# First chunk of an attention + expert-MLP kernel: second products in float32r from the fifth hidden tile, other places for two tiles' split weights, one subtraction moved to GpSimd

## The chip, the cores and the metric

One core of a Trainium2 chip runs the kernel. The metric is the device time in microseconds (us), median over runs of one build; an execution also has a profile, whose span (first to last recorded instruction) is a little shorter than its time.

## The reference

```python
scores = q @ k.T / sqrt(64)                      # 8 batches x 8 heads, 576 positions, head_dim 64
# heads 0-3: rel = pos_q - pos_k in [0, 32);  heads 4-7: rel in [0, 128) and rel % 4 == 0; else -1e9
attn = exp(scores - max) / (sum + 1e-9)
x = (attn @ v)  ->  (4608 tokens, 512)
h = x @ w_in                                     # 512 -> 2048
g = where(h > 0, h, exp(min(h, 0)) - 1)
out = g @ w_out                                  # 2048 -> 512
```

All inputs are float32 or wider; the MLP's weights come to the chip as 64-bit words.

## The kernel before

**Order of the work.** The attention of batch 0 is done first. Then the MLP goes through the tokens in chunks of 512 (chunks 0, 1 and 2), and what is left in larger pieces with combined weights. This case is about **chunk 0**, some 40 to 130 us into the span. It has 16 hidden tiles f = 0..15 of 128 features. For each f TensorE makes `product1(0, f)`, h = x times w_in of tile f, into one of two PSUM banks (`h0`, `h1`, in turn); ScalarE (ACT) and VectorE (DVE) make the ELU of it: ACT Exp (L627), ACT Relu (L629), DVE (L632 or L634). Two tiles later (`LAG` = 2) `second_product(0, f)` multiplies it with w_out of tile f and adds into four PSUM banks `o_ps0..3`. Attention of batch 1 (`second_attention`) runs between the tiles: scores into PSUM (`a_ps`), masks added by DVE (L397), maximum (L410, L413), Exp on ACT (L389), sums and reciprocal on DVE (L326, L327), the multiplication by them on GpSimd (POOL, L328), transposes on DVE (L432), copies into `pt` by ACT and POOL (L435), then products with v into `a_ps`.

**Weights.** A raw pair of weight tiles (w_in of one tile, w_out of another) is loaded into `r0`..`r3` and made float32 in `a0`..`a7`: ACT L136 (`magnitude`), then DVE L144, L152, L154 (`convert`, `upper_and_lower`).

**Two forms of a product.** In plain float32 one product is one matmul that TensorE runs in several passes. In float32r (F32R) each operand is split into a high part and a rest, and three matmuls (high·high, high·rest, rest·high) do the work. The split of a weight is `split_steps`: ACT casts (L191), a vector engine subtracts (L193). The split of an activation is `parts` in `elu`: ACT casts `gh` (L642), DVE subtracts `gl` (L643). First products of chunk 0 are float32r from f = `F1` = 3, second products from f = `F2` = 6. `split_w(k, t0, t1)` splits tile t0..t1 of pair k; called after tile f with k = f + 1 and t0 = 0 it splits w_in of tile f + 2, with t0 = 1 it splits w_out of tile f.

**Where the split weights go.** `places_of(k)` gives the two places: for k < 6 two buffers of a small pool (`brief`, of names `gl` or `h`), for 6 ≤ k < 8 a buffer `a-1`, later ones `r0` to `r2`. w_out of tiles below 11 goes to `brief("e")` or `brief("h")`.

**Order on the engines.** Matmuls keep the order of the program; on the other engines a scheduler fixes the order of the instructions when the kernel is built, from its own estimate of when each is ready (`schedule_with_timeline_sim=True`). On the chip each engine then runs its list strictly in order, and an instruction that waits holds all behind it. `tc.issue_after` adds a wanted order for single pieces.

Of the kernel before, what the change touches and what calls it, by code (L numbers as in the profile page):

```python
# [36 lines left out]
NE = 2  # L37
LAG = 2
F1 = 3
F2 = 6  # L40
NEG = -1.0e9
HT = DM // 2
TH = 384
# [31 lines left out]
def body(ctx: ExitStack, tc: tile.TileContext, q, k, v, masks, w_in, w_out, out):  # L75
    nc = tc.nc
# [82 lines left out]
    def room_of(name):  # L159

        if name not in taken:
            taken[name] = wst.tile([P, 4 if name[0] == "a" else 8, DM], F32 if name in PLAIN else F32R, name=name[:3].rstrip("'"))
        return taken[name]

    def slots(name, *at):

        step = at[1] - at[0] if len(at) > 1 else 1
        return room_of(name)[:, at[0]:at[-1] + 1:step, :]

    def brief(name):  # L170

        return [fp.tile([P, TC], F32R, name=name, bufs=4 if name == "e" else 2).unsqueeze(1) for _ in range(2)]

    def places_of(k, t0, t1):

        if k < 6:
            return brief("gl" if k % 2 else "h")
        if k < 8:
            o = (k - 6) * 2
            return slots("a-1", o), slots("a-1", o + 1)  # L180
        if k < 12:
            o = (k - 8) * 2
            return slots("r0", o), slots("r0", o + 1)
        o = k % 2 * 2
        return slots(f"r{1 + (k - 12) // 2}", o, o + 4), slots(f"r{1 + (k - 12) // 2}", o + 1, o + 5)

    def split_steps(k, t0, t1, places=None, v=nc.vector, a=nc.scalar):

        h, l = places or places_of(k, t0, t1)
        w = full2[k][:, t0:t1, :]  # L190
        a.copy(out=h, in_=w)  # L191
        yield
        v.tensor_tensor(out=l, in0=w, in1=h.bitcast(F32), op=ALU.subtract)  # L193
        for t in range(t0, t1):
            wh[need[2 * k + t]], wl[need[2 * k + t]] = h[:, t - t0, :], l[:, t - t0, :]

    def split_w(*args):

        for _ in split_steps(*args):
            pass  # L200
# [108 lines left out]
    def copies(b, hp, places, keep=lambda ins: ins):  # L309

        for a_ps, n0, n1 in places:
            flat, q0, q1 = a_ps[:, :(n1 - n0) * QB], n0 * QB, n1 * QB
            if hp >= NPAIR // 2:
                last = keep(nc.scalar.copy(out=x32[b][:, hp, q0:q1], in_=flat))
            else:
                dst = x32[b][:, hp, :].rearrange("p (c u) -> p c u", c=DIL)[:, :, q0 // DIL:q1 // DIL]
                last = keep(nc.scalar.copy(out=dst.rearrange("p c (s i) -> p s c i", i=G // DIL),
                                           in_=flat.rearrange("p (s c i) -> p s c i", c=DIL, i=G // DIL)))
        return last
# [258 lines left out]
    def split_x(c, v=nc.vector, a=nc.scalar, between=None):  # L578
        for hp in range(NC):
            if between is not None and hp == NC - 2:  # L580
                between()
            xh[hp], xl[hp] = xall[:, 2 * hp, :], xall[:, 2 * hp + 1, :]
            t0 = c * TC
            while t0 < (c + 1) * TC:
                b, o = divmod(t0, S)
                n = min(S - o, (c + 1) * TC - t0)
                u = slice(t0 - c * TC, t0 - c * TC + n)
                src = x32[b][:, hp, o:o + n]
                last_cast = a.copy(out=xh[hp][:, u], in_=src)
                last = v.tensor_tensor(out=xl[hp][:, u], in0=src, in1=xh[hp][:, u].bitcast(F32), op=ALU.subtract)  # L590
                t0 += n
        return last.ins, last_cast.ins
# [27 lines left out]
    def elu(h_ps, c, f, v=nc.vector, a=nc.scalar):  # L620
# [7 lines left out]
        if c == 0:  # L628
            below.append(nc.scalar.activation(out=e, in_=e, func=AF.Relu, scale=-1.0, bias=1.0).ins)  # L629
            if f < F2:  # L630
                g = fp.tile([P, TC], F32, name="gh", bufs=3)
# [353 lines left out]
    for c in range(CS):  # L985
        if c == 1:
            last_x = split_x(c, vec, act, lambda: copies(*last_outputs, inorder))
            pend.append((0, NF - 2, next(ends[0])))
            split_w(NF - 1, 0, 2, None, vec, act)
            next(ends[1])  # L990
            next(ends[1])
            pend.append((0, NF - 1, next(ends[1])))
            split = 1
        elif c > 1:
            split_x(c)
        if c == 1:
            for j in (14, 15, 12, 13, *range(12)):
                keep_whole(j)
        when = WHEN.get(c, ())
        for f in range(NF):  # L1000
            while c == 0 and ready < min(NF, f + AHEAD):
                for j in (ready, ready + 1):
                    with tc.issue_after(below[-1] if below else last_copy.ins):
                        magnitude(j)
                if f > 0:
                    with tc.issue_after(last_conversion.ins):
                        last_conversion = convert(ready // 2, behind=maxima[-1] if maxima else None)
                for j in (ready, ready + 1):
                    if j + 2 * NR < NF:
                        load_w(j + 2 * NR)  # L1010
                ready += 2
            if c == 0 and f == F1 - 2:
                with tc.issue_after(masked[-1] if masked else last_step[NPAIR - 1]), tc.issue_after(below[-1]):
                    split_x(0)
            while c == 1 and split < min(12, f + 2):
                with tc.issue_after(last_transpose[1] if split < 2 else last_x[0]), tc.issue_after(low[NF - 3 - F2] if split < 2 else last_x[1]):
                    with tc.issue_after(low[-1]), tc.issue_after(high[-1]):
                        split_late(split)
                split += 1
            strict = (vec, act) if c == CS - 1 and f >= LAST else ()  # L1020
            if c == 0 and f >= NF - 2:
                ends.append(elu_steps(gemm1(c, f)))
                if f == NF - 2:
                    next(ends[0])
                    first_late = split_steps(0, 0, 2, [slots(*a) for a in LATE[0]], vec, act)
                else:
                    for _ in first_late:
                        pass
                    next(ends[0])
            else:  # L1030
                parts = elu(gemm1(c, f), c, f, *strict)
                if parts is not None:
                    pend.append((c, f, parts))
            if c == 1:
                keep_plain(f)
            if (c, f) == (0, 0):

                for part in slice(0, 2 * DM), slice(2 * DM, 4 * DM):
                    with tc.issue_after(last_conversion.ins), tc.issue_after(hidden[-1]):
                        last_conversion = convert(1, part=part)  # L1040
            if c == 0 and F1 <= f + 2 < NF:

                with tc.issue_after(hidden[-2]):
                    split_w(f + 1, 0, 2 if f >= 11 else 1)
                    if F2 <= f < 11:
                        split_w(f + 1, 1, 2, brief("e" if f % 2 else "h"))
            if c == 0:
                with tc.issue_after(hidden[-1] if f > 1 else last_step[NPAIR - 1]):
                    last_outputs = next(att)
                if f == NF - 2:  # L1050
                    next(first_late)
            if (c, f) == (CS - 1, EARLY):
                made[0] = scores_piece(CS + 1, (0, 1), lambda: flush(LAG))
                credit[0] -= 6.0
            flush((LAG - 1 - (f == NF - 1) if c == 0 and f >= NF - 2 else LAG if c < CS - 1 or f < NF - 1 else LAG + 1) - len(waiting))
            if (c, f) in COMBINE:
                with tc.issue_after(low[-1]), tc.issue_after(high[-1]):
                    combine(COMBINE[c, f])
            if f in when:
                i = when.index(f)  # L1060
                if i % 2 == 0:
                    made[i] = scores_piece(c + 1, (i, i + 1))
                else:
                    outputs_piece(made.pop(i - 1))
            if (c, f) == (CS - 1, OPER):
                take_places()
                for what in SOON:
                    moving_operand(0, what, vec, act)
            if (c, f) == (CS - 1, OPER + 1):
                for what in THEN:  # L1070
                    moving_operand(0, what, vec, act)
# [67 lines left out]
```

## Time and profile before

| what | value |
|---|---|
| median of 3 runs | 872.69 us (871.42 to 872.86) |
| profiled execution | 872.5 us, span 870.7 us (1.8 us around it), mean granted clock 0.996 |
| TensorE (PE) busy | 853.7 us, 98% of the span |
| DVE, ACT, POOL busy | 555.7 (64%), 526.9 (61%), 75.0 us (9%) |

The profile has one row for each engine's instructions. In a timeline row the columns are the start in us from the span's start, the length of the group in us, the engine, the source line, the operation, what is written from what, the tile size, and the number of instructions in it. A square bracket at the end is the idle time of that engine ahead of the row, and what ended it. PE is TensorE's matmul stream.

### The profile page before, as it was taken

The numbers are of one execution on the slowest core, as the hardware profiler recorded it, in microseconds if no ns is written. First come the engines' busy times: TensorE is split into PE (matmuls) and PEld (weight loads), VectorE is DVE, ScalarE is ACT, GpSimd is POOL, SyncE is SP. The second block draws the span as 40 slices with busy tenths as digits, with TensorE's granted clock in tenths as the row PEclk, the third lists the DMA queues.
The fourth block names the chain that finished last, engine by engine and source line by source line (L and its number), as shares of the span: only waits on it lengthen the run. The fifth ranks groups of instructions, "written<-read, shape, count | busy, mean of one in ns | idle before, by whom it ended". The sixth has DMA issues, their size and how long they took to land.

```text
span 870.7 us, 17559 instructions
## 1 busy us (share of the span) xinstructions
PE 853.7 (98%) x6788; PEld 722.5 (83%) x6788; DVE 555.7 (64%) x902; ACT 526.9 (61%) x1031; POOL 75.0 (9%) x112
## 2 busy tenths in 40 slices
PE   6999999999999999999999999999999999999998
PEld 4556878888878889888878898988899988999986
DVE  6899987766685857787765577545476635344431
ACT  3767987756585756667654575654566654555541
POOL 2013311000020200111010020100011100000000
PEclk8999999999999999999999999999999999999999
DMA  9997335134546346867753867662875652776441
GB/s 343 378 381 264 132 123 188 34 132 133 176 160 200 102 151 215 262 221 239 231 173 100 279 200 242 212 184 83 265 226 175 206 164 80 241 209 191 143 153 56
DMA packets 93459, 166.48 MB, mean 191 GB/s; under 512 B 9696, under 2 KB 40768, under 8 KB 93376
## 3 DMA queue, kind: packets, MB, share of 16 engines
q1 hardware_dynamic: 89200, 158.01, 57.0%
q10 hardware_dynamic: 4176, 7.34, 2.3%
q8 instruction: 54, 0.88, 0.4%
q14 instruction: 29, 0.24, 0.1%
HBM read 124.42 MB, written 40.89 MB: 190 GB/s over the span
## 4 chain that ended last, share of the span: by engine, by line
PE 84%; DVE 7%; ACT 4%; DMA 2%; issue 2%; POOL 1%; SPq 0%; ACTq 0%; DVEq 0%; POOLq 0%
PE o_ps L111 41%; PE h L111 34%; PE a_ps L111 8%; DVE a L152 1%; DMA out<-e 1%; POOL pt L435 1%; DVE a L154 1%; DMA r<-combined 1%; DVE nmx L410 1%; ACT sm L389 0%; ACT pt L383 0%; DVE sm L397 0%; PE a L111 0%; DMA kt<-k 0%; DVE a L144 0%
## 5 line engine op out<-in xcount | busy, mean ns | idle before, releaser
L111 PE MATMUL h<-xall,r 128*128 128x384 f32 (+1 forms) x708 | 156.9, 363 | 0.4 <-DVE e L634 0.2
L111 PEld LDWEIGHTS h<-xall,r 128*128 128x128 f32 x708 | 127.7, 188 | 17.2 <-issue 0.8
L111 PE MATMUL o_ps<-a,gh 128*128 128x512 f32 x394 | 129.0, 416 | 0.0
L448 DVE SCALAR_TENSOR_TENSOR a-1_3369<-a-1_3369,a 128x768 f32<-128x768 f32 x64 | 61.0, 953 | 87.9 <-ACT a L448 87.9
L111 PE MATMUL h<-r,r 128*128 128x384 f32 x476 | 108.3, 337 | 0.4 <-DMA r<-combined 0.4
L448 ACT COPY e<-h 128x384 f32<-128x384 f32 x96 | 46.0, 479 | 98.5 <-PE h L111 96.6
L111 PEld LDWEIGHTS o_ps<-a,gh 128*128 128x128 f32 x394 | 73.4, 188 | 21.8 <-issue 9.1
L448 ACT ACTIVATE a<-a-1_3369 128x384 f32<-128x384 f32 (+1 forms) x96 | 60.8, 634 | 50.0 <-DVE a-1_3369 L448 44.0
L111 PEld LDWEIGHTS h<-r,r 128*128 128x128 f32 x476 | 84.4, 188 | 4.0 <-ACT e L448 0.7
L111 PE MATMUL o_ps<-r,gh 128*128 128x512 f32 x242 | 75.4, 393 | 0.0
L111 PE MATMUL o_ps<-a,r 128*128 128x512 f32 x288 | 72.3, 392 | 0.0
L111 PE MATMUL o_ps<-a,gl 128*128 128x512 f32 x173 | 67.7, 391 | 0.0
L448 ACT ACTIVATE a<-a 128x768 f32<-128x768 f32 (+1 forms) x72 | 60.8, 845 | 1.9
L111 PEld LDWEIGHTS o_ps<-a,r 128*128 128x128 f32 x288 | 53.7, 188 | 9.9
L111 PE MATMUL h<-a,r 128*128 128x384 f32 x256 | 60.1, 336 | 0.0
L448 DVE TENSOR_TENSOR a-1_3369<-h,e 128x384 f32<-128x384 f32 x64 | 35.2, 550 | 34.8 <-PE h L111 34.7
L111 PEld LDWEIGHTS o_ps<-r,gh 128*128 128x128 f32 x242 | 44.9, 188 | 8.6
L111 PEld LDWEIGHTS h<-a,r 128*128 128x128 f32 x256 | 46.4, 188 | 4.2
L111 PE MATMUL o_ps<-r,gl 128*128 128x512 f32 x117 | 46.0, 393 | 0.2 <-DVE gl L448 0.2
L435 POOL COPY pt<-sm 32x384 f32<-32x384 f32 x36 | 32.9, 913 | 103.1 <-DVE sm L432 102.1
L111 PE MATMUL o_ps<-a,xall 128*128 128x512 f32 x153 | 39.5, 393 | 0.0
L637 DVE SCALAR_TENSOR_TENSOR e<-h,e 128x512 f32<-128x512 f32 x30 | 20.9, 696 | 27.1 <-ACT e L636 27.1
(219 smaller groups left out, 1553.6 us busy)
## 6 DMA issues: line engine op xcount, KB each, us to landing
r<-combined SPq DMA_DIRECT2D x224, 256.0 KB, 3.6
aside<-a-1_3369 SPq DMA_DIRECT2D x64, 192.0 KB, 3.4
vt<-v SPq DMA_DIRECT2D x30, 384.0 KB, 4.4
kt<-k SPq DMA_DIRECT2D x30, 304.0 KB, 4.9
qt<-q SPq DMA_DIRECT2D x30, 288.0 KB, 4.2
r<-w_in SPq DMA_DIRECT2D x16, 512.0 KB, 7.9
r<-w_out SPq DMA_DIRECT2D x16, 512.0 KB, 8.3
combined<-a SPq DMA_DIRECT2D x20, 256.0 KB, 3.2
```

Source lines behind the costliest of these rows:

```text
L111: return inorder(nc.tensor.matmul(*args, **kw))
L152: keep(nc.vector.scalar_tensor_tensor(out=au, in0=hi, scalar=0x80000000, in1=au, op0=ALU.bitwise_and, op1=ALU.bitwise_or))
L154: return keep(nc.vector.scalar_tensor_tensor(out=au, in0=lo, scalar=29, in1=au, op0=ALU.logical_shift_right, op1=ALU.bitwise_or))
L410: nc.vector.tensor_reduce(out=nmx, in_=sm, op=ALU.max, axis=mybir.AxisListType.X)
L435: last_transpose[b] = (nc.gpsimd.tensor_copy if r else nc.scalar.copy)(out=tr[ks, :, cs], in_=sm[cs, :, rs]).ins
L448: return lambda *args, **kw: inorder(getattr(self.eng, name)(*args, **kw))
L637: v.scalar_tensor_tensor(out=e, in0=h_ps, scalar=0.0, in1=e, op0=ALU.max, op1=ALU.subtract)
```

## The change

`F2` goes from 6 to 4, so second products of tiles 4 and 5 are float32r too; their w_out is split into a buffer that later holds `a6` (`slots("a6''", ...)`). The splits of w_in of pairs k < 6 go into a buffer that later holds `a7` (`slots("a7''", ...)`) and no longer into the pool's. The subtraction for w_in of the fourth tile (f = 3, called after tile 1 = `F1` - 2) is issued to GpSimd and no longer to DVE.

```diff
-F2 = 6
+F2 = 4
...
         if k < 6:
-            return brief("gl" if k % 2 else "h")
+            o = k % 2 * 2
+            return slots("a7''", o), slots("a7''", o + 1)
...
                 with tc.issue_after(hidden[-2]):
-                    split_w(f + 1, 0, 2 if f >= 11 else 1)
+                    split_w(f + 1, 0, 2 if f >= 11 else 1, None, nc.gpsimd if f == F1 - 2 else nc.vector)
                     if F2 <= f < 11:
-                        split_w(f + 1, 1, 2, brief("e" if f % 2 else "h"))
+                        o = f % 2 * 2
+                        split_w(f + 1, 1, 2, (slots("a6''", o), slots("a6''", o + 1)) if f < 6 else brief("e" if f % 2 else "h"))
```

In the built program line numbers grow by 1 below L176 (by 2 in the last lines). Three places show how the order on the engines moves. Numbers behind names tell buffers apart.

**DVE, tiles 3 to 5**, from the ELU of tile 3 to that of tile 5 (`gh`, `e` by L632/L633, L634/L635: the ELU; `a2`, `a3`: weights being converted; L193/L194: rests of weights; `sm`, `a_ps`: attention). Before:

```order
L632 SCALAR_TENSOR_TENSOR gh_704<-h1_688,e_701 128x512
L144 TENSOR_SCALAR a3_769<-a3_769 128x2048
L193 TENSOR_TENSOR h_707<-a2_638,h_706 128x512
L193 TENSOR_TENSOR gl_799<-a2_638,gl_798 128x512
L432 STREAM_TRANSPOSE sm_619<-sm_619 96x12x32 x2
L632 SCALAR_TENSOR_TENSOR gh_796<-h0_780,e_793 128x512
L397 TENSOR_TENSOR sm_748<-a_ps0_710,masks_sb_76 96x384
L397 TENSOR_TENSOR sm_748<-a_ps1_711,masks_sb_76 96x384
L632 SCALAR_TENSOR_TENSOR gh_839<-h1_823,e_836 128x512
```

With the change:

```order
L633 SCALAR_TENSOR_TENSOR gh_701<-h1_685,e_698 128x512
L144 TENSOR_SCALAR a3_764<-a3_764 128x2048
L194 TENSOR_TENSOR a7_577<-a2_637,a7_577 128x512
L194 TENSOR_TENSOR a6_798<-a2_637,a6_798 128x512
L433 STREAM_TRANSPOSE sm_618<-sm_618 96x12x32 x2
L194 TENSOR_TENSOR a7_577<-a2_637,a7_577 128x512
L635 SCALAR_TENSOR_TENSOR e_788<-h0_775,e_788 128x512
L644 TENSOR_TENSOR gl_793<-e_788,gh_792 128x512
L398 TENSOR_TENSOR sm_743<-a_ps0_705,masks_sb_76 96x384
L398 TENSOR_TENSOR sm_743<-a_ps1_706,masks_sb_76 96x384
```

Between the ELU of tile 4 and the mask additions now stands `gl` of tile 4 (and ACT's cast for it), and one more rest lies ahead.

**DVE, tiles 10 and 11**, where `gl_1133` (before) and `gl_1153` (with the change) belong to tile 10, `gl_1172` and `gl_1192` to tile 11. Before:

```order
L634 SCALAR_TENSOR_TENSOR e_1128<-h0_1115,e_1128 128x512
L193 TENSOR_TENSOR h_1139<-a5_990,h_1138 128x512
L154 SCALAR_TENSOR_TENSOR a6_1109<-r2_644,a6_1109 128x2048
L643 TENSOR_TENSOR gl_1133<-e_1128,gh_1132 128x512
L634 SCALAR_TENSOR_TENSOR e_1167<-h1_1154,e_1167 128x512
L397 TENSOR_TENSOR sm_1216<-a_ps0_1178,masks_sb_76 96x384
L397 TENSOR_TENSOR sm_1216<-a_ps1_1179,masks_sb_76 96x384
L144 TENSOR_SCALAR a7_1249<-a7_1249 128x2048
L193 TENSOR_TENSOR r1_1175<-a6_1109,r1_1175 128x2x512
L410 TENSOR_REDUCE nmx_1219<-sm_1216 96x12
L193 TENSOR_TENSOR r1_1175<-a6_1109,r1_1175 128x2x512
L643 TENSOR_TENSOR gl_1172<-e_1167,gh_1171 128x512
```

With the change:

```order
L194 TENSOR_TENSOR h_1159<-a5_1010,h_1158 128x512
L154 SCALAR_TENSOR_TENSOR a6_1129<-r2_643,a6_1129 128x2048
L635 SCALAR_TENSOR_TENSOR e_1148<-h0_1135,e_1148 128x512
L635 SCALAR_TENSOR_TENSOR e_1187<-h1_1174,e_1187 128x512
L398 TENSOR_TENSOR sm_1236<-a_ps0_1198,masks_sb_76 96x384
L398 TENSOR_TENSOR sm_1236<-a_ps1_1199,masks_sb_76 96x384
L144 TENSOR_SCALAR a7_1269<-a7_1269 128x2048
L194 TENSOR_TENSOR r1_1195<-a6_1129,r1_1195 128x2x512
L411 TENSOR_REDUCE nmx_1239<-sm_1236 96x12
L194 TENSOR_TENSOR r1_1195<-a6_1129,r1_1195 128x2x512
L644 TENSOR_TENSOR gl_1153<-e_1148,gh_1152 128x512
L644 TENSOR_TENSOR gl_1192<-e_1187,gh_1191 128x512
```

`gl` of tile 10 moves from ahead of the mask additions to behind both wide rests, directly ahead of `gl` of tile 11.

**ACT, start of chunk 1** (`L624 COPY h<-h0` takes h of a tile out of the one PSUM bank that chunk 1 uses for it; L418 is the Exp of an attention; L678 copies results out). Before:

```order
L642 CAST gh_1662<-e_1497 128x512
L191 CAST a6_1695<-a1_538 128x1024
L624 COPY h_1660<-h0_1646 128x512
L627 ACTIVATE e_1659<-h_1660 128x512
L678 COPY e_1674<-o_ps0_680 128x512
L418 ACTIVATE sm_1593<-sm_1593 96x768
L678 COPY e_1680<-o_ps1_682 128x512
```

With the change:

```order
L643 CAST gh_1682<-e_1517 128x512
L192 CAST a6_1715<-a1_538 128x1024
L419 ACTIVATE sm_1613<-sm_1613 96x768
L625 COPY h_1680<-h0_1666 128x512
L628 ACTIVATE e_1679<-h_1680 128x512
L679 COPY e_1694<-o_ps0_677 128x512
L679 COPY e_1700<-o_ps1_679 128x512
```

The attention's Exp now stands ahead of the copy of h of tile 1 of chunk 1; before it stood three instructions behind it.

## Rows read from the trace of the kernel before

**Rows 1.** The page: busy time by engine, and the busy tenths of PE and DVE in 40 equal slices of the span (21.8 us each).

```profile
PE 853.7 (98%) x6788; PEld 722.5 (83%) x6788; DVE 555.7 (64%) x902; ACT 526.9 (61%) x1031; POOL 75.0 (9%) x112
...
PE   6999999999999999999999999999999999999998
...
DVE  6899987766685857787765577545476635344431
```

**Rows 2.** Busy time by stretch of chunk 0. Columns: stretch, length, busy us (and instructions) of PE, PEld, DVE, ACT, POOL, then granted clock, DMA share, GB/s.

```profile
44.00:62.00 18.00, 16.96 (x126) 10.38 (x124) 16.77 (x21) 11.91 (x37) 2.97 (x4) 1.00 1.01 378
62.00:84.00 22.00, 21.71 (x161) 13.69 (x160) 21.25 (x24) 18.31 (x48) 5.80 (x3) 1.00 0.79 281
84.00:113.00 29.00, 29.00 (x214) 23.57 (x213) 27.29 (x34) 22.29 (x54) 9.55 (x6) 1.00 0.44 147
113.00:135.00 22.00, 21.77 (x132) 17.24 (x131) 17.94 (x28) 18.85 (x54) 3.52 (x4) 1.00 0.34 109
```

**Rows 3.** Timeline of PE, tiles 3 to 7: the first product of tile 3 (in two rows, the wait between them), the attention's product with v, then first product of tile 6, second of tile 4, first of tile 7, second of tile 5.

```profile
44.48 2.11 PE L111 MATMUL h<-xall,h 128*128 128x512 f32 x8
47.63 1.19 PE L111 MATMUL h<-xall,h 128*128 128x512 f32 x4 [1.03 <-DVE h L193]
...
62.56 1.23 PE L111 MATMUL a_ps<-pt,vt 128*64 128x96 f32 x24 [0.29 <-PE h L111]
...
66.85 3.31 PE L111 MATMUL h<-xall,gl 128*128 128x512 f32 x12
70.00 3.59 PE L111 MATMUL o_ps<-a,gh 128*128 128x512 f32 x8
73.03 3.30 PE L111 MATMUL h<-xall,a-1_841 128*128 128x512 f32 x12
...
77.16 3.70 PE L111 MATMUL o_ps<-a,gh 128*128 128x512 f32 x8
```

**Rows 4.** Timeline of PE, second products of tiles 10 (from 107.80) and 11 (from 113.24), with the first use of `gl` in each, and first products of tiles 13 and 14.

```profile
107.80 0.61 PE L111 MATMUL o_ps<-h,gh 128*128 128x512 f32 x2
108.25 0.39 PE L111 MATMUL o_ps<-h,gl 128*128 128x512 f32 x1
...
110.52 2.88 PE L111 MATMUL h<-xall,r 128*128 128x512 f32 x12
113.24 0.62 PE L111 MATMUL o_ps<-r,gh 128*128 128x512 f32 x2
113.70 0.39 PE L111 MATMUL o_ps<-r,gl 128*128 128x512 f32 x1
...
116.38 3.01 PE L111 MATMUL h<-xall,r 128*128 128x512 f32 x12 [0.23 <-DVE e L634]
```

**Rows 5.** Timeline of DVE: the maximum and the rest around 45 us, ELU of tile 4, mask additions, `gl` of tile 10, the ELU of tile 11 directly behind it, and `gl` of tile 11; the brackets are all waits of DVE over 0.2 us from 44.30 to 112.78.

```profile
44.30 0.94 DVE L410 TENSOR_REDUCE nmx<-sm 96x12 f32<-96x768 f32 x1
...
46.89 0.68 DVE L193 TENSOR_TENSOR h<-a,h 128x512 fp32r<-128x512 f32 x1
...
60.06 0.65 DVE L632 SCALAR_TENSOR_TENSOR gh<-h,e 128x512 f32<-128x512 f32 x1
61.91 1.02 DVE L397 TENSOR_TENSOR sm<-a_ps,masks_sb 96x384 f32<-96x384 f32 x2 [1.20 <-POOL pt L435]
63.60 0.69 DVE L632 SCALAR_TENSOR_TENSOR gh<-h,e 128x512 f32<-128x512 f32 x1 [0.67 <-ACT e L629]
...
85.66 1.02 DVE L397 TENSOR_TENSOR sm<-a_ps,masks_sb 96x384 f32<-96x384 f32 x2 [0.95 <-POOL pt L435]
...
95.75 0.69 DVE L634 SCALAR_TENSOR_TENSOR e<-h,e 128x512 f32<-128x512 f32 x1 [0.65 <-ACT e L629]
...
106.38 0.68 DVE L643 TENSOR_TENSOR gl<-e,gh 128x512 fp32r<-128x512 f32 x1
106.98 0.68 DVE L634 SCALAR_TENSOR_TENSOR e<-h,e 128x512 f32<-128x512 f32 x1
...
112.78 0.67 DVE L643 TENSOR_TENSOR gl<-e,gh 128x512 fp32r<-128x512 f32 x1
```

**Rows 6.** Timeline of POOL in chunk 0: two multiplications of the attention, tensor operations with two inputs.

```profile
55.43 1.47 POOL L328 TENSOR_TENSOR sm<-sm,sums 96x768 f32<-96x768 f32 x1 [35.05 <-DVE sums L327]
...
94.55 1.89 POOL L328 TENSOR_TENSOR sm<-sm,sums 96x768 f32<-96x768 f32 x1 [8.92 <-DVE sums L327]
```

**Rows 7.** Timeline of DVE: an instruction that lies beside the first of these, and one of the same kind that has none of POOL's multiplications beside it.

```profile
55.72 2.26 DVE L144 TENSOR_SCALAR a<-a 128x2048 uint32<-128x2048 uint32 x1
...
80.80 1.20 DVE L144 TENSOR_SCALAR a<-a 128x2048 uint32<-128x2048 uint32 x1
```

**Rows 8.** Timeline of ACT: the cast of w_in of tile 3, the first conversion for `a6`, and three rows of the start of chunk 1.

```profile
43.81 0.62 ACT L191 CAST h<-a 128x512 fp32r<-128x512 f32 x1 [1.15 <-DVE a L154]
...
95.62 2.16 ACT L136 ACTIVATE a<-r 128x1024 f32<-128x1024 f32 x2
...
140.51 0.59 ACT L624 COPY h<-h 128x512 f32<-128x512 f32 x1 [0.69 <-PE h L111]
...
143.13 0.85 ACT L418 ACTIVATE sm<-sm 96x768 f32<-96x768 f32 x1 [0.89 <-DVE sm L417]
143.88 0.56 ACT L678 COPY e<-o_ps 128x512 f32<-128x512 f32 x1
```

**Rows 9.** Timeline of PE: first product of tile 2 of chunk 1.

```profile
143.03 2.88 PE L111 MATMUL h<-xall,r 128*128 128x512 f32 x12
```

## The prediction

> **What bounds the kernel now.** Read first the busy shares [rows 1]: PE is busy 98% of the span, so the program as a whole is bound by TensorE, and a saving of matmul time counts unless something else is late. The slices in tenths in the same group speak against reading the change off that average: DVE stands at 9, 9, 8, 7, 7, 7 and 6 in the slices from the third on, which is chunk 0, and at 3 to 5 at the end. The table by stretch shows it closer [rows 2]: DVE is busy 16.77 of 18.00 us, 21.25 of 22.00 and 27.29 of 29.00, that is 93 to 97% up to 113 us; PE in the same stretches loses 1.04, 0.29 and 0 us. Two engines are full there, and PE is the one that sets the pace only by a little. How little is seen by following DVE to where PE uses its results: PE uses `gl` of tile 11 at 113.70, and DVE had it ready at 112.78 + 0.67 = 113.45, 0.25 us earlier; `gl` of tile 10 was ready at 107.06 and used at 108.25, 1.19 us earlier [rows 4, 5]. So the question is less what PE is spared than what DVE gets to do between 44 and 113 us, and in which order.
>
> The predicted sum is made against the profiled execution, 872.5 us, 0.2 us below the median of the three runs (872.69). About 0.2%, 1.74 us, is what a measurement of this kernel can tell from no change.
>
> **The change, part by part.**
>
> *A. Second products of tiles 4 and 5 in float32r: PE −1.5 us.* A first product and the float32 second product after it take 73.03 − 66.85 = 6.18 us [rows 3]; a second product in float32r and the first product after it 113.24 − 107.80 = 5.44 us [rows 4]. That spares 0.74 us a tile, 1.48 us for two.
>
> *B. The fourth tile's rest on GpSimd: the wait of 1.03 us goes, and comes back 15 us later: 0.* PE waits 1.03 us at 46.6 for DVE's rest of w_in of tile 3, which DVE only makes at 46.89 [rows 3, 5]. GpSimd is idle there and can start when ACT's cast ends, 43.81 + 0.62 = 44.43 [rows 8]. No subtraction of this size by GpSimd is in the trace; its multiplications of 96x768 took 1.47 to 1.89 us [rows 6], so for 512 elements per partition in place of 768 I estimate 0.98 to 1.26 us, and take 0.98; as bounds stand 0.6 (DVE's own pace) and the whole 1.89. Even at 1.89 the rest is there at 46.3, before PE needs it at 44.48 + 2.11 = 46.59. So the wait goes. But at 62.56 the attention's product with v had already to wait 0.29 us, and it writes the banks that DVE's mask additions read until half of 1.02 us behind 61.91, i.e. 62.42 [rows 3, 5]. PE can come there a microsecond earlier; it only gains if the mask additions do too. In the new order DVE's transposes end one subtraction (0.60 us, the step from 106.38 to 106.98) earlier, but then come one more rest, the ELU of tile 4 (done at about 60.7, as now at 60.06 + 0.65), then `gl` of tile 4, which has to wait for ACT's cast of 0.62 us: 60.7 + 0.1 + 0.62 = 61.4, plus 0.67 for itself, gives 62.05 as the start of the mask additions in place of 61.91. Nothing is gained there: B is 0 for the span.
>
> *The places: 0.* The buffer of `a6` is wanted by ACT's conversion only at 95.62 [rows 8], that of `a7` later; the last readers of the new places are the first product at 66.85 and the second product at 77.16 [rows 3], which end some 15 us and more before. Were that cover gone, the conversion of 2.16 us, and ACT's casts behind it, would wait for them. No DMA is added or removed. ACT's four more casts of 0.62 us (`gh` of tiles 4 and 5, w_out of 4 and 5), 2.5 us, are hidden in the 6.1 us it idles from 44 to 62 and the 3.7 us from 62 to 84 [rows 2], but for the one cast above.
>
> *C. DVE has more to do, and `gl` of tile 10 is put last: +5.8 us.* DVE gets four subtractions (rests of w_out 4 and 5, `gl` of 4 and 5) and loses one (w_in of tile 3). I count by the lists of instructions. From the maximum at 44.30 on, what stands ahead of `gl` of tile 10 in the new list is what stood ahead of `gl` of tile 11 in the old one, plus one rest and one `gl` of 128x512 (the other two of the four take the place of the w_in rest that went and of `gl` of tile 10 itself). So `gl` of tile 10 starts where tile 11's did, 112.78, plus 2 × 0.60 = 1.20, plus the change in DVE's waits. Those were 1.20 + 0.67 + 0.95 + 0.65 = 3.47 us [rows 5]. In the new order I expect 0.75 (`gl` of tile 4 behind its cast, above; the first two waits go, since the work now lies in them), 0.95 (as before), and 1.3 at the transposes near 96, which wait for GpSimd's multiplication of 1.89 us [rows 6] with only one ELU of 0.6 between: together about 3.05, 0.4 less. `gl` of tile 10 then starts at 112.78 + 1.20 − 0.4 = 113.6 and is ready at 114.25; PE can use it at 114.3. Before it used it at 108.25. PE therefore is 6.06 us late at that place, whatever it gained ahead of it (A and B only make the wait there longer). Of this 0.23 us comes back, since before's wait of 0.23 at 116.38 [rows 4] is covered then. Net +5.8 us. Bounds: if all of DVE's waits vanished, `gl` would start at 112.78 + 1.20 − 3.47 = 110.5 and be used at 111.2, +2.9 and net +2.7; if all stayed as before and DVE lost 0.6 more beside GpSimd, 114.6 as a start, 115.3 as use, +7.1 and net +6.8. I take 5.8, nearer the upper end, because the rows with the waits are ones that the new order keeps or replaces by like ones.
>
> *D. Start of chunk 1: ACT's Exp ahead of a copy: +1.5 us.* Chunk 1 has one PSUM bank for h, so the first product of tile 2 waits for ACT's copy of tile 1's h. Before, that copy ran at 140.51 to 141.10, and the product at 143.03 didn't wait [rows 8, 9]. Now the Exp of an attention, which waited for DVE and ran at 143.13 to 143.98, stands ahead of it. The copy would take the slot behind it, 143.88 to 144.47, and the product start at 144.5 in place of 143.03. Bounds: 0 (the Exp ready earlier relative to PE, as PE comes late into this chunk by C) and 143.88 − 140.51 = 3.4 (the copy late by that, nothing hidden). I take 1.5.
>
> Sum: 872.5 + 5.8 + 1.5 = **879.8 us**; the ends of C and D give 875.2 (with 2.7 and 0) to 882.7 (with 6.8 and 3.4). Late next behind C is tile 11: its `gl` comes directly behind, so it costs nothing more.
>
> *A rule weighed.* By the rows, DVE does wait beside GpSimd: L144 took 2.26 us at 55.72, while GpSimd multiplied from 55.43 to 56.90, and 1.20 us at 80.80 with no multiplication beside it [rows 6, 7]. The Trainium skill, page "SBUF — State Buffer", section "Who interferes with whom", says that a DVE instruction with two SBUF inputs contends with a GpSimd instruction that reads SBUF, and that whoever is first holds the shared ports for the whole instruction while the other is blocked; the rows agree. By that rule the moved subtraction, if it lasts to 45.5, blocks nothing, and if to 46.3, it holds DVE's conversion at 45.76 for 0.5 us: the sum would be 879.8 or 880.3.
>
> **Rivals.**
>
> *Faster: PE sets the pace all the way (870.0 us).* If DVE keeps up, A and B are kept: 872.5 − 1.48 − 1.03 = 870.0. It is one mechanism, DVE's lead over PE at tile 10: it decides by whether `gl` of tile 10 is ready when PE, 2.5 us earlier, wants it, 108.25 − 2.5 = 105.75. For it: PE's saving is sure, and DVE loses a rest early. Against: DVE's slack at tile 11 was 0.25 us, three subtractions net come on top, and the order puts `gl` of tile 10 behind 5.8 us of work that was behind it before (106.98 to 112.78). Chance 0.11.
>
> *Level: only the added work counts, not the order (872.9 us).* If the waits give DVE room, so that it is at `gl` of tile 10 in time, and only tile 11 is late: ready at 112.78 + 1.20 − 0.4 + 0.67 = 114.25 with 114.31 as first use against 113.70: +0.6, less the 0.23: 872.9. For it: this is where the backlog alone would hit. Against: each engine runs its list in order, so the place of `gl` of tile 10 counts. Chance 0.09.
>
> *Heavier (883 to 886 us).* GpSimd and DVE hold each other up as in [rows 7] (0.5 to 1), D goes to its 3.4, and what ACT does for chunk 1 is late once more (1 to 3). 872.5 + 6.8 + 3.4 = 882.7 and above. Chance 0.10.
>
> *The change does nothing*, because float32r in tiles 4 and 5 is hidden anyway, is in the level case.
>
> **How the numbers follow.** Forecast 0.70 (879.8; its own range 875.2 to 882.7), faster 0.11, level 0.09, heavier 0.10. The range leaves out the faster case, half of the level one and the upper part of the heavier one, some 2 in 10: 873.0 to 883.5. Faster by over 0.2%: 0.11; within it: 0.09; slower: 0.80.
>
> **What would show it.** In the changed profile: no wait of PE at 46.6, and a GpSimd subtraction of 128x512 of about 1 us from 44.5 on (B); PE waiting 0.3 to 1.5 us ahead of the product with v near 62.6, for DVE (B is 0); second products of tiles 4 and 5 in rows of two and one float32r matmuls in place of one row of x8 (A); DVE at 95% or more between 44 and 113; the largest wait of PE in chunk 0, some 3 us, at the first use of `gl` of tile 10 near 113 to 114 (C); a wait of PE of 1 to 2 us for ACT's copy in chunk 1, near 150 (D). C is wrong if that wait isn't there, or if tile 10's second product has begun its third matmul before 111; D is wrong if no wait for L625 is over 0.5 us beyond before's.

## The result, and the profile after

| | median | runs | ratio to before (95% interval) |
|---|---|---|---|
| before | 872.74 us | 871.42 to 872.86 | |
| with the change | 883.34 us | 882.9 to 884.47 | 1.0122 (1.0106 to 1.0138) |

The change makes the kernel 10.6 us slower; 879.8 was predicted, with a range of 873.0 to 883.5. The measured time lies 0.16 us below the upper end of that range. The profiled execution took 882.9 us, its span is 881.1 us, 10.4 more than before.

The page of the changed kernel, busy time by engine and the busy tenths of PE and DVE, answers to [rows 1]:

```profile
PE 856.4 (97%) x6796; PEld 725.6 (82%) x6796; DVE 558.9 (63%) x905; ACT 530.1 (60%) x1035; POOL 72.3 (8%) x113
...
PE   6989989999999999999999999999999999999998
...
DVE  6899977757585866787765476645466646344331
```

In chunk 0, PE has two slices of 8 now where it had 9. The table by stretch answers to [rows 2]:

```profile
44.00:62.00 18.00, 17.60 (x126) 10.37 (x124) 17.95 (x21) 12.64 (x38) 4.66 (x4) 1.00 1.01 382
62.00:84.00 22.00, 19.81 (x159) 14.26 (x160) 21.06 (x25) 17.41 (x47) 5.46 (x6) 0.92 0.77 261
84.00:113.00 29.00, 26.79 (x201) 20.78 (x199) 27.69 (x34) 24.90 (x59) 4.80 (x5) 1.00 0.47 162
113.00:135.00 22.00, 19.68 (x108) 15.73 (x110) 14.82 (x20) 13.03 (x42) 3.27 (x4) 0.92 0.29 96
```

DVE is busy 17.95 of 18.00 us and 21.06 of 22.00, PE stands still for 2.2 to 2.3 us in each of the three later stretches, and the granted clock, 1.00 throughout before, is 0.92 on the mean in two of them. The timeline of PE shows where (all its waits of over 0.2 us in chunk 0, with the rows behind two of them, and the two at the start of chunk 1), to be read against [rows 3, 4, 9]:

```profile
47.19 1.21 PE L111 MATMUL h<-xall,a 128*128 128x512 f32 x4 [0.22 <-POOL a L194]
...
64.19 1.26 PE L111 MATMUL a_ps<-pt,vt 128*64 128x96 f32 x24 [2.36 <-DVE sm L398]
65.37 5.30 PE L111 MATMUL o_ps<-a,gh 128*128 128x512 f32 x8
70.11 3.32 PE L111 MATMUL h<-xall,a 128*128 128x512 f32 x12
...
105.52 0.50 PE L111 MATMUL o_ps<-e,gl 128*128 128x512 f32 x1 [0.78 <-DVE gl L644]
...
108.93 3.06 PE L111 MATMUL h<-xall,r 128*128 128x512 f32 x12 [0.86 <-DVE e L635]
111.82 0.61 PE L111 MATMUL o_ps<-h,gh 128*128 128x512 f32 x2
115.32 0.50 PE L111 MATMUL o_ps<-h,gl 128*128 128x512 f32 x1 [2.88 <-DVE gl L644]
...
118.84 3.36 PE L111 MATMUL h<-xall,r 128*128 128x512 f32 x12
122.04 0.61 PE L111 MATMUL o_ps<-r,gh 128*128 128x512 f32 x2
...
152.50 3.06 PE L111 MATMUL h<-xall,r 128*128 128x512 f32 x12 [1.08 <-ACT h L625]
...
159.36 3.01 PE L111 MATMUL h<-xall,a 128*128 128x512 f32 x12 [1.07 <-ACT h L625]
```

The second product at 65.37 takes 4.74 us up to the next row, where the same one took 66.85 − 63.72 = 3.13 in the kernel before:

```profile
63.72 3.70 PE L111 MATMUL o_ps<-a,gh 128*128 128x512 f32 x8
```

Busy time hides this: PE counts as busy for the whole of the 4.74 us. The table in stretches of 1 and 2 us behind the two long waits shows the clock (third number from the end):

```profile
65.00:66.00 1.00, 1.00 (x11) 0.71 (x8) 0.96 (x2) 1.00 (x2) 0.00 (x0) 0.61 0.65 232
66.00:67.00 1.00, 1.00 (x2) 0.34 (x1) 0.99 (x2) 1.00 (x4) 0.00 (x0) 0.50 0.50 98
67.00:68.00 1.00, 1.00 (x2) 0.34 (x1) 1.00 (x1) 1.00 (x8) 0.00 (x0) 0.50 0.75 272
...
116.00:118.00 2.00, 2.00 (x8) 1.53 (x7) 2.00 (x3) 1.50 (x7) 0.00 (x0) 0.60 0.18 60
118.00:120.00 2.00, 2.00 (x7) 1.57 (x6) 1.59 (x3) 2.00 (x14) 0.00 (x0) 0.54 0.03 8
120.00:122.00 2.00, 2.00 (x10) 1.68 (x9) 2.00 (x2) 1.11 (x8) 0.00 (x0) 1.00 0.00 0
```

About a microsecond after each of the two waits the clock goes from 2.4 to 1.2 GHz (0.50), for some 3.5 us. What the other engines did there: GpSimd's subtraction, DVE's conversion beside it, `gl` of tile 4, the mask additions, `gl` of tiles 10 and 11; and ACT at the start of chunk 1 (answering to [rows 5, 8]):

```profile
44.85 2.28 POOL L194 TENSOR_TENSOR a<-a,a 128x512 fp32r<-128x512 f32 x1 [24.13 <-ACT a L192]
```

```profile
46.10 2.11 DVE L152 SCALAR_TENSOR_TENSOR a<-r,a 128x1024 uint32<-128x1024 uint32 x1
...
62.75 0.71 DVE L644 TENSOR_TENSOR gl<-e,gh 128x512 fp32r<-128x512 f32 x1 [0.68 <-ACT gh L643]
63.39 1.01 DVE L398 TENSOR_TENSOR sm<-a_ps,masks_sb 96x384 f32<-96x384 f32 x2
...
114.58 1.28 DVE L644 TENSOR_TENSOR gl<-e,gh 128x512 fp32r<-128x512 f32 x2
```

```profile
151.13 0.84 ACT L419 ACTIVATE sm<-sm 96x768 f32<-96x768 f32 x1 [3.79 <-DVE sm L418]
151.89 0.56 ACT L625 COPY h<-h 128x512 f32<-128x512 f32 x1
```

`gl` of tiles 10 and 11 run back to back from 114.58, with no idle time of DVE ahead of them. ACT stands 3.79 us behind DVE, and the copy that PE needs stands behind that Exp.

**How late PE is, mark by mark.** TensorE's products come in the same order in all kernels here (f adds twelve matmuls to one of them), so a product's start can be set against its start in the trace of before. The table gives the difference in us, less the difference at 44.48 (which lies ahead of the change and is −0.1 to 1.0).

| start in before, and what starts | change | a | b | c | e | f | g | h | j | k |
|---|---|---|---|---|---|---|---|---|---|---|
| 62.56 product with v | 1.28 | 0.86 | 0.41 | 0.42 | 1.28 | 1.29 | 0.70 | 0.30 | 0.00 | 0.00 |
| 66.85 first product 6 | 2.91 | 0.84 | 0.41 | 0.42 | 2.96 | 2.92 | 0.70 | 0.30 | 0.00 | −0.01 |
| 107.80 second product 10 | 3.67 | 2.31 | 0.41 | 0.46 | 3.68 | 3.62 | 0.29 | −0.01 | 1.01 | 1.04 |
| 113.24 second product 11 | 8.45 | 7.48 | 0.41 | 2.17 | 3.68 | 6.84 | 4.25 | −0.01 | 2.67 | 1.04 |
| 140.31 chunk 1, behind first product 1 | 7.88 | 6.93 | −0.14 | 1.61 | 4.79 | 6.27 | 3.67 | 1.13 | 2.12 | 2.43 |
| 154.39 chunk 1, first product 4 | 10.18 | 7.12 | −0.34 | 1.14 | 7.71 | 8.57 | 3.95 | 0.65 | 1.64 | 2.62 |

In the column of the change, 4.8 us come from second product 10 to second product 11 (the wait and the half clock behind it), and 2.3 at the start of chunk 1. Behind 154.39 it stays as it is.

### The profile page after: what moved, and what is told of

It reads as the page before. It is cut to its first block, busy times and chain, and to the rows that moved or that the text cites. A ratio compares the mean times of both kernels' runs of the same rounds, so it can differ in the third digit from the quotient of the medians.

```text
span 881.1 us, 17581 instructions
## 1 busy us (share of the span) xinstructions
PE 856.4 (97%) x6796; PEld 725.6 (82%) x6796; DVE 558.9 (63%) x905; ACT 530.1 (60%) x1035; POOL 72.3 (8%) x113
## 4 chain that ended last, share of the span: by engine, by line
PE 85%; DVE 6%; ACT 5%; issue 2%; DMA 1%; SPq 0%; POOL 0%; ACTq 0%; DVEq 0%
PE o_ps L111 41%; PE h L111 35%; PE a_ps L111 8%; DVE a L152 1%; DMA kt<-k 1%; DVE a L144 1%; ACT pt L384 0%; DVE sm L398 0%; ACT sm L390 0%; DVE a L194 0%; DVE nmx L411 0%; ACT a L136 0%; ACT pt L436 0%; ACT gh L643 0%; ACT a L192 0%
## 5 line engine op out<-in xcount | busy, mean ns | idle before, releaser
L111 PE MATMUL o_ps<-a,gl 128*128 128x512 f32 x181 | 70.8, 391 | 0.0
L111 PEld LDWEIGHTS o_ps<-a,gl 128*128 128x128 f32 x181 | 34.0, 188 | 7.1
```

The source lines that it names most:

```text
L111: return inorder(nc.tensor.matmul(*args, **kw))
```

## The experiments

The theory (L): PE is set by when DVE reaches `gl` of tile 10 in its list; then come the half clock behind long waits and ACT's list at the start of chunk 1. Its rivals put the loss on GpSimd (G), on the amount of DVE's work alone (W), on PE's lost time adding up from the front (P), or on the places.

**a: the rest of tile 4 on DVE again.**

```diff
-                    split_w(f + 1, 0, 2 if f >= 11 else 1, None, nc.gpsimd if f == F1 - 2 else nc.vector)
+                    split_w(f + 1, 0, 2 if f >= 11 else 1)
```

> The change with the subtraction of the fourth tile's rest back on DVE. Theory L (the list of DVE): the time is set by where DVE's list puts the gl of tile 10, and by what PE's long waits cost behind it; GpSimd's part is small. DVE gets 0.60 us back to do and loses the 0.90 us that its conversion was held at 46.1. PE's largest wait of chunk 0, near 112 to 115, stays over 2 us. 881 to 885 us. Rival G (GpSimd): the subtraction on GpSimd, 2.28 us where 0.98 was estimated, and the hold of DVE beside it make most of the loss; without it 873 to 877 us.

Measured: 879.4 us, ratio 1.0073 (1.0055 to 1.0092). Both numbers missed. The rows of PE, of DVE's L152 and of ACT:

```profile
114.62 0.67 PE L111 MATMUL o_ps<-h,gl 128*128 128x512 f32 x1 [3.29 <-DVE gl L644]
```

```profile
46.34 1.23 DVE L152 SCALAR_TENSOR_TENSOR a<-r,a 128x1024 uint32<-128x1024 uint32 x1
```

```profile
148.04 0.59 ACT L625 COPY h<-h 128x512 f32<-128x512 f32 x1 [1.41 <-PE h L111]
...
149.94 0.85 ACT L419 ACTIVATE sm<-sm 96x768 f32<-96x768 f32 x1 [0.18 <-DVE sm L418]
```

Chunk 0 went as L had it: the wait at tile 10 stays, 6.93 of 7.88 us are left in the table's fifth line. What was not foreseen is that the scheduler now put the copy ahead of the Exp again, and the start of chunk 1 costs 0.2 us in place of 2.3. So this run also bears on the last term of the sum: with the Exp ahead of the copy the last step of the table costs 2.3 (the change and f) and 2.9 (e), with the copy ahead 0.3 or less (a, b, c, g, h, j, k; 0.7 in d). No run moves that Exp alone. Of the 3.06 us by which a is ahead of the change at 154.39 (7.12 against 10.18), 2.1 come from this order and 0.95 were there at 140.31 already.

**b: GpSimd's subtraction alone**, and **d: the new places of w_in alone**, each in the kernel before.

```diff
# b
-                    split_w(f + 1, 0, 2 if f >= 11 else 1)
+                    split_w(f + 1, 0, 2 if f >= 11 else 1, None, nc.gpsimd if f == F1 - 2 else nc.vector)
# d
-            return brief("gl" if k % 2 else "h")
+            o = k % 2 * 2
+            return slots("a7''", o), slots("a7''", o + 1)
```

> The kernel before with only the fourth tile's subtraction on GpSimd. Theory L: PE's wait of 1.03 us at 46.6 shrinks to some 0.2, DVE's conversion next to it is held 0.9 us and DVE has 0.6 us less to do; nothing is gained at the product with v near 62.6, since the mask additions come no earlier. 871.5 to 874 us. Rival G: DVE's hold of 0.9 us is carried on to tile 10 and 11, where DVE had 0.25 us of slack, and long waits follow: 876 us or more.

> The kernel before with only the other places for the split w_in of pairs below 6 (second products still float32r from tile 6, subtraction on DVE). Theory L: nothing waits for the new places, DVE's list keeps its order: 871.5 to 874 us. Rival: the places are not free in time, or the writes into them cost elsewhere: 875 us or more.

Measured: b 872.56 us, ratio 1.0 (0.999 to 1.001); d 873.23 us, 1.0003 (0.9994 to 1.0012). Two rows of PE in b:

```profile
46.85 1.19 PE L111 MATMUL h<-xall,h 128*128 128x512 f32 x4 [0.24 <-POOL h L193]
...
62.98 1.23 PE L111 MATMUL a_ps<-pt,vt 128*64 128x96 f32 x24 [1.51 <-issue]
```

PE's wait of 1.03 us [rows 3] becomes 0.24, and the 0.29 us at the product with v becomes 1.51: the gain is waited off there, as term B had it. Neither part costs by itself what the change costs. The place in `a6` for w_out has no run of its own.

**c: the whole change with second products in float32r from tile 5 on.**

```diff
-F2 = 4
+F2 = 5
```

> The change with float32r second products from the sixth tile on in place of the fifth (tile 5 only). DVE's list puts the gl of tile 10 behind the mask additions and one conversion, but ahead of both wide rests. Theory L: ahead of it stand 2.7 us of DVE's work that stood behind it before, plus 0.6 for one subtraction net, plus 0.9 for the hold, less some 0.8 of waits: it is ready near 110.5 in place of 107.1, PE waits for it 1.5 to 2.5 us; with 0 to 2 us at the start of chunk 1 this gives 874 to 878 us. If the number of subtractions alone counted and not the place in the list, 873 us or less; if the cost came from GpSimd alone, the same as the whole change, 881 to 885.

Measured: 875.75 us, ratio 1.0036 (1.0022 to 1.0049), inside L's range. PE waits 1.37 us at `gl` of tile 10, a little under the 1.5 to 2.5 expected; the clock stays at 1.00. The time alone says less than it seems to: of the 3.3 us by which this span is longer than before's, only 1.1 are there at 154.39. The rest comes later, a part of it at waits of 0.46 to 0.60 us for a DMA, and is not explained.

**e: `gl` of tile 10 early**, the same work.

```diff
-                    with tc.issue_after(below[-1] if below else last_copy.ins):
+                    with tc.issue_after(high[10 - F2] if f == 12 else below[-1] if below else last_copy.ins):
                         magnitude(j)
...
-                with tc.issue_after(hidden[-2]):
+                with tc.issue_after(low[10 - F2] if f in (11, 12) else hidden[-2]):
...
-                with tc.issue_after(hidden[-1] if f > 1 else last_step[NPAIR - 1]):
+                with tc.issue_after(hidden[-1] if f > 1 else last_step[NPAIR - 1]), tc.issue_after(low[-2] if f == 11 else hidden[0]):
                     last_outputs = next(att)
```

> The change with the gl of tile 10 put ahead, on DVE, of both wide rests, the mask additions and the conversion (on ACT its cast ahead of the conversion of a7); TensorE's list and the amount of work stay the same. Theory L: DVE makes it directly behind the ELU of tile 11, ready near 111.7, before PE wants it at 112.3. PE's wait of 2.88 us goes, and with it the 3.6 us at half clock behind it (1.7 us). 883.3 - 4.6 = 878.7, between 877 and 880.5 us. Rival W (the amount of DVE's work): the gl of tile 11 or the ELU of tile 12 is late by as much instead, 882 us or more.

Measured: 880.51 us, ratio 1.0091 (1.0074 to 1.0108), at the upper end of L's range and below W's 882. PE has no wait at tile 10 and no half clock behind it:

```profile
111.63 0.62 PE L111 MATMUL o_ps<-h,gh 128*128 128x512 f32 x2
112.09 0.39 PE L111 MATMUL o_ps<-h,gl 128*128 128x512 f32 x1
```

The table's delay stays at 3.68 where the change goes from 3.67 to 8.45. But a part comes back at an attention product, whose probabilities now are later, since their mask additions stand behind `gl`:

```profile
131.18 1.21 PE L111 MATMUL a_ps<-pt,vt 128*64 128x96 f32 x24 [1.65 <-POOL pt L436]
```

So the place in the list is what set the 4.8 us at tile 10, but not all of it is a gain at the end: 1.65 us come back at this product and some 0.6 at the start of chunk 1, so that the kernel is only 2.8 us faster than with the change (880.51 against 883.34).

**f: TensorE kept busy through the wait**, with matmuls whose output nothing reads.

```diff
         for m, (a, w) in enumerate(terms):
+            if (c, f, t, m) == (0, 10, 0, 2):
+                idle_ps = ps_a.tile([P, TC], F32, name="a_ps0")
+                for _ in range(12):
+                    mm(idle_ps, gh[:, :P], wh[i], start=True, stop=True)
```

> The change with twelve more float32r matmuls of 128x512 (12 x 0.227 = 2.7 us, into a PSUM bank that nothing reads) right where TensorE waits 2.88 us for the gl of tile 10. The lists of the other engines stay the same. Theory C (the clock falls because TensorE stood still): the wait is filled, the granted clock stays at 1.0 near 116 to 120, and the second product and the first product behind it take 1.7 us less: 881 to 882.5 us although work was added. Rival: the clock falls for another reason, or costs nothing since other engines are late: 883 us or more.

Measured: 882.39 us, ratio 1.0109 (1.0093 to 1.0124), against 1.0122 (1.0106 to 1.0138) of the change: the intervals overlap, so the verdict is read from the trace:

```profile
111.81 2.88 PE L111 MATMUL a_ps<-h,gh 128*128 128x512 f32 x12
114.91 0.50 PE L111 MATMUL o_ps<-h,gl 128*128 128x512 f32 x1 [0.21 <-DVE gl L644]
...
120.02 0.62 PE L111 MATMUL o_ps<-r,gh 128*128 128x512 f32 x2
```

```profile
116.00:118.00 2.00, 2.00 (x11) 1.65 (x10) 2.00 (x3) 1.92 (x10) 0.00 (x0) 1.00 0.04 9
118.00:120.00 2.00, 2.00 (x10) 1.68 (x9) 2.00 (x3) 2.00 (x14) 0.00 (x0) 1.00 0.00 0
```

From the first use of `gl` to second product 11 it takes 120.02 − 114.91 = 5.11 us, in the change 122.04 − 115.32 = 6.72: 1.6 us less for the same products. Only the wait was filled and the clock stayed up, so at this place it falls because TensorE stood still. The 1.6 us are still there at 154.39 (8.57 against 10.18); later this trace has waits of its own of 0.76 us at 396.60 and 1.20 at 634.49, with no releaser shown, in attention pieces.

**g: the mask additions ahead of `gl` of tile 4.**

```diff
-            low.append(v.tensor_tensor(out=gl, in0=e, in1=gh.bitcast(F32), op=ALU.subtract).ins)
+            with tc.issue_after(masked[-1] if (c, f) == (0, 4) else high[-1]):
+                low.append(v.tensor_tensor(out=gl, in0=e, in1=gh.bitcast(F32), op=ALU.subtract).ins)
```

> The change with the gl of tile 4 put behind the attention's mask additions on DVE, in place of ahead of them. Theory L: the mask additions come some 1.3 us earlier, PE's wait at the product with v (2.36 us near 64) falls to 1 or 1.5 us, and the 3.5 us at half clock behind it go with it; but all that only makes PE wait longer for the gl of tiles 9 and 10, which come when DVE is there. 881.5 to 884 us. Rival P (PE's lost time adds up from the front): 880 us or less.

Measured: 877.11 us, ratio 1.0044 (1.0029 to 1.0059): missed by 4 us, and rival P's number came true. It is not a clean test. With this one wish the scheduler gave DVE another list, above all from tile 8 on, in which the last mask additions and their maximum stand behind `gl` of tile 10, and ACT has the copy ahead of the Exp. PE's delay ahead of tile 10 is 0.29 us in place of 3.67; its wait at 64 is 1.77 us, without half clock behind it; the one at tile 10 is 2.04 us, with it. How much of that is the early mask addition and how much the new list stays open.

**h: a, g and e together** (their three diffs in one kernel).

> The change with the rest of tile 4 on DVE, the mask additions ahead of the gl of tile 4, and the gl of tile 10 early; with these lists ACT's Exp at the start of chunk 1 stands behind the copy, as in the kernel before. Theory L: of a_rest_on_dve (879.4) the wait of 3.29 us at tile 10 and the 1.7 us at half clock behind it go, waits of 0.8 us at tiles 9 and 11 stay: 873.5 to 876 us. Rival W: the work that DVE has more makes other waits of the same size, 878 us or more. A version faster than before (under 871.5) would need DVE never to be last.

Measured: 875.13 us, ratio 1.0032 (1.0018 to 1.0045), inside L's range and below W's 878. So the three together take back 8.2 of the 10.6 us. No wait at tile 10, no half clock; one of 1.69 us, for `pt`, at the attention product of 128.12.

**j and k: half of the change (`F2 = 5`, all rests on DVE), with the list as the scheduler makes it (j) and with e's wishes (k).** j is the diffs of a and c together, k those of a, c and e.

> Half of the change and without GpSimd: float32r second products from the sixth tile on, all rests on DVE. Against c_f2_5 (875.75, before 873.18) DVE makes one subtraction more (0.6 us) and isn't held (0.9 us). Theory L: 0.3 us less at the gl of tile 10, where PE waited 1.37 us; PE's wait near 46.6 is back but absorbed: 874.5 to 875.8 us, 1.3 to 2.6 above before. Rival G (GpSimd makes the loss): level with before or faster, 873.5 or less.

> As j_f2_5_dve, with the gl of tile 10 put ahead of the attention's mask additions and of the conversion on DVE. Theory L: PE's wait at the gl of tile 10 goes (0 to 0.4 us are left), the amount of work is the same: 872 to 874 us, that is level with the kernel before, since 0.74 us of TensorE's time is spared and other waits of about that size stay. Rival W (the amount of DVE's work sets the time, wherever it stands): the same as j_f2_5_dve within 0.5 us.

Measured: j 874.68 us, ratio 1.0022 (1.0013 to 1.0031); k 874.29 us, 1.0018 (1.0009 to 1.0028). j is inside L's range and above the 873.5 of rival G. In k the 1.37 us at tile 10 are gone, and the attention product waits:

```profile
128.50 1.21 PE L111 MATMUL a_ps<-pt,vt 128*64 128x96 f32 x24 [1.62 <-POOL pt L436]
```

k came out 0.3 us above its range, and within 0.4 of j, which is what rival W had said. So the place in the list decides where PE waits and, with the whole change, whether the clock falls (in j it stays at 1.00 too); once that is mended, h, j and k are still 1.5 to 2.2 us slower than the kernel before. That this rest is DVE's added work is not tested by itself. No version was faster than the kernel before.

## Why the prediction was right, and where it was short

The sign, the bound (DVE's list) and the places of the large waits were right; the sum was some 3 us short (+7.3 forecast, +10.6 measured, +10.4 in the two spans). That the time stayed inside the range is in part luck: it is above the 882.7 that the forecast gave itself, and inside the 883 to 886 of the heavier rival, of whose three parts two came (the hold beside GpSimd, and a second late copy of ACT in chunk 1), while the largest missing piece, the clock, was neither in the forecast nor in that rival. By term:

- **A, forecast −1.48.** Measured in the table's own marks: the delay falls by 0.73 us over tile 4's second product (from 73.27 − 70.00 = 3.27 to 78.80 − 76.26 = 2.54) and as much over tile 5's. Right, and in the change without effect on the end, since PE waits at tile 10 for something later than itself.
- **B, forecast 0, the wait gone.** The wait went to 0.22 and the gain was waited off at the product with v; b shows it alone. The price was mis-sized: GpSimd took 2.28 us, in the other traces 2.27 or 2.28, where 0.98 was taken and 1.89 was the upper bound. The bound came from another operation, a multiplication with a broadcast operand and another output type, and it was no bound even for that: the same multiplication took up to 2.90 us in g and h. With it came what the port rule was weighed for: DVE's L152 at 46.10 took 2.11 us, in a, with no GpSimd beside it, 1.23. That is the heavier rival's mechanism: 0.9 us, taken as 0 in the sum (C's upper bound had 0.6 for it).
- **The rule.** L152 ended at 48.21, 1.08 us behind GpSimd's subtraction (47.13), where it takes 1.23 alone: nearly as if it had begun then. The Trainium skill, page "SBUF — State Buffer", section "Who interferes with whom", says that a DVE instruction with two SBUF inputs contends with a GpSimd instruction that reads SBUF, and that the one issued first blocks the other; these rows agree. The L144 of [rows 7], on which the prediction rested it, has one input in SBUF, so that only L152 tests the part on two inputs.
- **C, forecast +5.8.** `gl` of tile 10 was used at 115.32 − 0.35 (the start's shift) = 114.97 against 108.25: +6.72 where 6.06 was forecast. Of the 0.66, 0.90 is the hold; DVE's waits were 0.68 + 0.21 + 0.23 + 0.89 = 2.01 us where 3.05 was expected, which gives 1.0 back (the prediction's own three terms add up to 3.00, not 3.05); some 0.8 us are left. A part of them are longer instructions between 82 and 104 (five took 0.3 us more than others of their kind, in the kernel before three did); this was not followed further. Right in mechanism, 0.7 short.
- **The missing term.** Behind the wait of 2.88 us TensorE ran at half clock, 1.73 us more than before from the first use of `gl` to second product 11 (6.72 against 4.99). No wait of before in this stretch was over 1.03 us and its clock stood at 1.00, so the forecast had no row for it; f shows it. The same at 65 to 69 cost 1.6 us there; it should have cost nothing in the end, since PE waited at tile 10 anyway, but no run tests that by itself.
- **Give-back, forecast −0.23**, measured 7.88 − 8.45 = −0.57.
- **D, forecast +1.5, bounds 0 to 3.4.** Measured 10.18 − 7.88 = +2.3, in two waits of 1.08 and 1.07, of which the forecast saw one.

6.72 + 1.73 − 0.57 + 2.3 = 10.18, and with the shift of 0.35 at the start and 0.17 us given back later the 10.4 of the spans.

One reading of the rows was wrong as well: from the third slice on, the tenths of DVE in [rows 1] are 9, 9, 9, 8, 7, 7 and 6, not 9, 9, 8, 7, 7, 7 and 6. Nothing hangs on it, since the sum goes by the stretches of [rows 2].

Not foreseen either was the wait at the product with v: 2.36 us where 0.3 to 1.5 was given. The mask additions began at 63.39 − 0.35 = 63.04 in place of 62.05, late by 1.0 us, about the hold.

## What to carry to other kernels

When TensorE is busy 98% of the span, look at which engine delivers with the least slack before sparing matmul time: a cheaper matmul that asks for more operand preparation moves the work to the engine that is already last. Count the instructions ahead of each deadline in that engine's list, since an instruction's place can cost more than its length: `gl` of tile 10 takes 0.6 us of DVE's time, its place cost 4.8 us at tile 10, and with that place alone mended the kernel was 2.8 us faster. The other waits have to be mended with it, since what one gives back the next can take (e against h). And price a long new wait above its own length where it may lower TensorE's clock.

## What the runs showed of the hardware that was not expected

- TensorE's waits of chunk 0 over 1.3 us that were followed by half clock in these traces: 2.04, 2.36, 2.37, 2.88 and 3.29 us; not followed by it: 1.37, 1.50, 1.51, 1.62, 1.65, 1.69 and 1.77 us. Each time the half clock lasted 3 to 4 us and cost 1.6 to 1.75 where it could be timed.
- A subtraction of 128x512 float32 into float32r takes GpSimd 2.27 to 2.28 us in the six traces that have it there, and DVE about 0.68, and DVE's conversion with two operands in SBUF that was issued meanwhile took 2.10 to 2.13 in place of 1.22.
